# A transformer block's first attention block, paced by a fixed list of steps over 32 score pairs

## The chip, the core and the metric

The kernel runs on one core of one Trainium2 chip. Its time is device microseconds (us) for one launch. Three runs of the kernel before gave 1453.79, 1454.96 and 1455.0 us; their median, 1454.96 us, is what the change is compared with. Lower is better.

## The reference, cut to what matters

One transformer block on 2048 tokens of width 512: layer norm, attention with 32 query heads of 16 columns that share one key and one value head, a residual, layer norm again, a gated feed-forward part of width 1792, and a second residual.

```python
q = (x @ wq).reshape(B, S, H, Dh)          # x is the layer-normed input
k = x @ wk;  v = x @ wv                    # one K and one V head for all 32 query heads
scores = einsum("bhqd,bkd->bhqk", q, k) * (Dh ** -0.5)
o = einsum("bhqk,bkd->bhqd", softmax(scores), v)
h = x + o.reshape(B, S, H * Dh) @ wo
out = h + (gelu(ln(h) @ w_gate) * (ln(h) @ w_up)) @ w_down
```

All inputs and outputs are float32. The kernel splits most operands into a high and a low part, so that one projection takes three matmuls (high by high, high by low, low by high) for each 128 rows of depth.

## The kernel before, in words

The 2048 queries are cut into four blocks of 512 (`NB`, `T`). A prologue normalizes the input, makes K and V for all tokens and most of the queries of block 0. Then attention runs block by block. In a block there are 8 groups of four heads (`NG`), and in a group 16 chunks of 128 keys (`KC`). One chunk is two *score pairs*: `score(n)` (line 774) issues two matmuls into one score tile of PSUM (line 329) and one `exp` on ScalarE over 128x1024 scores (line 333). So a group is 32 score pairs and a block 256. There are three score tiles: two named `s` and, in the first block, a third (`s3`, line 324). ScalarE writes its result into an SBUF tile `p`, one for each chunk, of which there are five (`PB`).

A chunk whose two pairs are issued goes into the list `pend`. `finish(k)` (line 753) takes up to k chunks from its front and issues their *V-products* (`weigh`, line 335): four products of 512 columns, each of which the profile shows as two matmul instructions, so 8 for a chunk. All 16 chunks of a group add into one PSUM bank `acc`, of which there is one. After a group's last chunk `evacuate` (line 348) copies it on VectorE into `oT` (line 350), which leaves by DMA; a later DMA brings it back turned, and VectorE inverts the sums (line 366) and makes the split outputs `o_hi` and `o_lo`. Those steps wait in the list `outs` and are taken by `take_out`.

While block 0 attends, two more things are done beside it.

- The queries of blocks 1 to 3, and the rest of block 0, are projected by the generator `project_q` (line 170). Each 128 columns of `wq` (a piece `c`, four of them in a block) take 12 matmuls into one PSUM bank (`pq`; `width = 1`, so there is one such bank). The generator gives the word back after every three matmuls. After the last three, VectorE splits the bank into `qh` and `ql`, squares it into `qs`, and three DMAs on SyncE's queue store them. For the pieces in `HURRY` the bank is first copied to SBUF (`pq_raw`) and split from there. After a block's four pieces come the norm matmuls (`pqn`, line 218), which need all four `qs`, a copy `qn` and a maximum on VectorE, four small steps on GpSimd (`mm`, lines 227 to 234) and a last VectorE step `m` (line 245) that waits for them.
- `part_weights` (line 406) halves, splits and stores the feed-forward weights in 46 steps, all on GpSimd and its DMA queue. Their order in the program follows the score pairs (one step after every fourth pair but every 24th), but nothing in them waits for TensorE.

TensorE, ScalarE, VectorE, GpSimd and SyncE run in program order there, so the loop at line 811 sets what stands behind what. It works in fours of score pairs. Before the fourth pair of each four, if projection work is left, the generator is asked once: three matmuls, or a block's norm step. At the start it is asked twice before each of pairs 4, 6 and 8 (`RAMP`). After the fourth pair `finish` issues the V-products of all chunks but two, which is two chunks at a time. When no work is left, `finish(1)` also runs after the second pair of each four, so that the chunks go one by one.

The loop runs over block 0 and the first 16 pairs of block 1 (`lead`, 272 pairs). At pair 256 `drain` issues whatever projection work is left, the early tiles are closed, and four pairs later `dense(0)`, the output projection and feed-forward part of block 0, is set up. From pair 272 on a second loop (line 857) runs attention of blocks 1 to 3 with the dense work of the block before woven in, by fixed shares. The last dense block runs alone.

Of the kernel before, what the change touches and what calls it, by code (L numbers as in the profile page):

```python
# [29 lines left out]

HURRY = ((0, 3), (1, 0), (1, 1))

RAMP = {3: 2, 5: 2, 7: 2}

RUNS = ((0, 1, 2, 3), (4, 5, 6, 7), (8, 9, 10, 11), (12, 13))

# [6 lines left out]
def kernel(  # L43
# [23 lines left out]
    DC = D // P  # L67
    FC = F // P
    NG = H // 4
    KC = S // P  # L70
# [35 lines left out]
    def split(eng_hi, hi, lo, src, eng_lo=None):  # L106
        if eng_hi is nc.scalar:
            nc.scalar.activation(hi, src, AF.Copy)
        else:
            eng_hi.tensor_copy(hi, src)  # L110
        (eng_lo or nc.vector).tensor_tensor(lo, src, hi.bitcast(F32), op=ALU.subtract)  # L111
# [29 lines left out]
    def run(outer, first):  # L141
# [10 lines left out]
        def psum1(name):  # L152
            return ps.tile([P, T], F32, tag="d", bufs=width, name=name)
# [16 lines left out]
        def project_q(b, cs, eng, col):  # L170
            tsl = slice(b * T, (b + 1) * T)
            xT_hi, xT_lo = xT[b]
            urgent = b == 0 and cs[0] == 0
            qss = []
            for c in cs:
                pq = psum1(f"pq_{b}_{c}")
                n = 0
                for d in range(DC):
                    for wt, xt in ((wq_hi, xT_hi), (wq_hi, xT_lo), (wq_lo, xT_hi)):
                        nc.tensor.matmul(  # L180
                            pq, wt[:, d, c * P : (c + 1) * P], xt[:, d, :],
                            start=(n == 0), stop=(n == 3 * DC - 1),
                        )
                        n += 1
                    if urgent or d < DC - 1:
                        yield 3

                raw = None
                if (b, c) in HURRY:
                    raw = eb.tile([P, T], F32, tag="vT", bufs=3, name=f"pq_raw_{b}_{c}")  # L190
                    if b == 0:
                        nc.scalar.activation(raw, pq, AF.Copy)
                    else:
                        nc.vector.tensor_copy(raw, pq)
                    yield 3
                qh = eb.tile([P, T], F32R, tag="qh", bufs=2, name=f"qh_{b}_{c}")
                ql = eb.tile([P, T], F32R, tag="ql", bufs=2, name=f"ql_{b}_{c}")
                if raw is not None:
                    split(nc.vector, qh, ql, raw)
                else:  # L200

                    split(nc.vector if b == 0 and c == FIRST_Q else eng, qh, ql, pq)
                qs = eb.tile([P, T], BF16, tag="qs", bufs=DC, name=f"qs_{b}_{c}")
                (nc.gpsimd if urgent else nc.vector).tensor_tensor(
                    qs, qh.bitcast(F32), qh.bitcast(F32), op=ALU.mult
                )
                qss.append(qs)
                for r0, part in ((0, qh), (DH, ql), (2 * DH, qh)):
                    nc.sync.dma_start(
                        q_d[c * HC : (c + 1) * HC, r0 : r0 + DH, tsl].bitcast(F32),  # L210
                        part.bitcast(F32),
                    )
                if raw is None or b == 0:
                    yield 3

            pn = psum1(f"pqn_{b}_{cs[0]}")[:H, :]
            for i, c in enumerate(cs):
                nc.tensor.matmul(
                    pn, sel[:, c, :], qss[i], start=(i == 0), stop=(i == len(cs) - 1)
                )  # L220
            qn = eb.tile([H, T], F32, tag="qn", bufs=1, name=f"qn_{b}_{cs[0]}")
            nc.vector.tensor_copy(qn, pn)
            nc.vector.tensor_reduce(q2[:, col : col + 1], qn, axis=AX.X, op=ALU.max)
            yield 2

            mm = eb.tile([H, 3], F32, tag="mm", bufs=2, name=f"mm_{b}_{cs[0]}")
            nc.gpsimd.tensor_scalar(
                mm[:, 0:1], q2[:, col : col + 1], k2m, 1e-30, op0=ALU.mult, op1=ALU.add
            )
            nc.gpsimd.tensor_tensor(mm[:, 1:2], mm[:, 0:1], power[:H, 0:1], op=ALU.pow)  # L230
            nc.gpsimd.tensor_scalar(
                mm[:, 2:3], mm[:, 0:1], mm[:, 1:2], 0.5, op0=ALU.mult, op1=ALU.mult
            )
            nc.gpsimd.tensor_scalar(
                mm[:, 1:2], mm[:, 1:2], k2m, 0.5, op0=ALU.mult, op1=ALU.mult
            )
            m = eb.tile([H, T], F32R, tag="m", bufs=2, name=f"m_{b}_{cs[0]}")
            if urgent:
                nc.scalar.activation(
                    m, qn, AF.Identity, bias=mm[:, 2:3], scale=mm[:, 1:2]  # L240
                )
                ms[b] = m
                return
            yield 0
            nc.vector.tensor_scalar(m, qn, mm[:, 1:2], mm[:, 2:3], op0=ALU.mult, op1=ALU.add)
            hs = slice(cs[0] * HC, (cs[-1] + 1) * HC)
            nc.sync.dma_start(q_d[hs, 3 * DH, tsl].bitcast(F32), m[hs].bitcast(F32))
            yield 2
# [4 lines left out]

        def later_q():
            second = project_q(1, range(DC), nc.vector, 1)
            for _ in range(sum(RAMP.values())):
                yield next(second)

            next(q_rest)
            for _ in range(2 * DC - sum(RAMP.values())):  # L260
                yield next(second)
            yield from q_rest
            yield from second
            for b in range(2, NB):
                yield from project_q(b, range(DC), nc.vector, b)
            check_bound(eb, k2m)
# [68 lines left out]
        def weigh(acc, p, kc):  # L335
            for j in range(4):
                nc.tensor.matmul(  # L337
                    acc[32 * j : 32 * j + 32, :], v_sb[:, kc, :], p[:, j, :],
                    start=(kc == 0), stop=(kc == KC - 1), skip_group_check=True,
                )  # L340
# [63 lines left out]
        db = None  # L404
# [342 lines left out]
        PER = NG * KC  # L747
        work = None
        qgs = {(0, 0): qg_first if first else load_q(0, 0)}
        acc = None  # L750
        pend = []

        def finish(n):
            for _ in range(min(n, len(pend))):
                pb, pg, pkc, pp, pacc, _ = pend.pop(0)
                weigh(pacc, pp, pkc)
                if pkc == KC - 1:
                    evacuate(pb, pg, pacc)
# [44 lines left out]
        n, lead = 0, 2 * PER + sum(SIZES[: LEAD[0]])  # L803
        with tc.manual_schedule(engines={mybir.EngineType.SP, mybir.EngineType.DVE}):
            parts = None
            if first:
                work = later_q()
                parts = part_weights(early.enter_context(tc.tile_pool(name="parts", bufs=1)))


            while n < lead:
                if n == 2 * PER:
                    drain()
                    for _ in parts or ():
                        pass
                    parts = None
                    early.close()
                    db = late.enter_context(tc.tile_pool(name="dense", bufs=1))
                if n % 4 == 0:
                    given = work is not None  # L820
                for _ in range(RAMP.get(n, n > 7 and n % 4 == 3) if given else 0):
                    if next(work, None) is None:
                        work = None
                score(n)
                n += 1
                if n % 4 == 2 and not given and len(pend) > 2:
                    finish(1)
                if n % 4:
                    continue
                if len(pend) > 2:  # L830
                    finish(len(pend) - 2)
                if outs:
                    take_out()
                if parts is not None and n > 12 and n % 24:
                    next(parts, None)
                if n == 2 * PER + 4:
                    primed = dense(0)
                    next(primed)
        assert not outs
        work = primed  # L840
        set_banks("ps_rest")
# [15 lines left out]
        for c in range(LEAD[0], (NB - 1) * NG * len(SIZES)):  # L857
            b, cb = divmod(c, NG * len(SIZES))
# [4 lines left out]
            if b > 0 and cb == LEAD[b]:  # L863
                assert work is None
                work, todo = dense(b), list(kinds)
# [34 lines left out]
            if work is not None and not todo:  # L900
                assert next(work, None) is None
                work = None
# [259 lines left out]
    def check_bound(sb, k2m):  # L1162
        q2m = sb.tile([H, 1], F32, name="q2m")
        nc.vector.tensor_reduce(q2m, q2, axis=AX.X, op=ALU.max)
        nc.vector.tensor_tensor(q2m, q2m, k2m, op=ALU.mult)
        nc.sync.dma_start(b_d.rearrange("o h -> h o"), q2m)
# [77 lines left out]
```

## Time and profile before

The profiled execution took a span of 1453.0 us on the core; the median of the runs is 1454.96 us, so some 2 us lie outside the span or between executions.

| | before |
|---|---|
| median of 3 runs | 1454.96 us |
| span of the profiled execution | 1453.0 us |
| chain that ended last: TensorE / ScalarE / GpSimd / DMA | 65% / 16% / 6% / 5% |
| HBM read / written | 131.13 MB / 47.71 MB |
| mean granted TensorE clock | 0.998 |
| exp on ScalarE (line 333) | 1024 times, 969.0 us busy |
| V-products on TensorE (line 337) | 4096 instructions, 490.7 us busy |
| scores on TensorE (line 329) | 1984 instructions beside the 64 of the first group, 394.0 us busy |

How to read the views used below. The page's first part gives for each engine its busy time and the number of its instructions. A timeline row has the start and the length in us, the engine, the line of the kernel, the operation, the tiles written and read, their shapes, how many instructions were merged into the row, and in brackets how long the engine had been idle and whose result it then waited for. "PE" is TensorE's matmuls, "DVE" VectorE, "ACT" ScalarE, "POOL" GpSimd, "SPq" SyncE's DMA queue. Matmul lengths overlap with the next matmul, so that the time of a run of them is read from start to start. In a row of the score line, x2 is one score pair; in a row of the V-products, x8 is one chunk. A row of stretches gives start and end, the length, and then busy time and instructions of each engine.

### The profile page before, as it was taken

The numbers are of one execution on the slowest core, as the hardware profiler recorded it, in microseconds if no ns is written. First come the engines' busy times: TensorE is split into PE (matmuls) and PEld (weight loads), VectorE is DVE, ScalarE is ACT, GpSimd is POOL, SyncE is SP. The second block draws the span as 40 slices with busy tenths as digits, with TensorE's granted clock in tenths as the row PEclk, the third lists the DMA queues.
The fourth block names the chain that finished last, engine by engine and source line by source line (L and its number), as shares of the span: only waits on it lengthen the run. The fifth ranks groups of instructions, "written<-read, shape, count | busy, mean of one in ns | idle before, by whom it ended". The sixth has DMA issues, their size and how long they took to land.

```text
span 1453.0 us, 24765 instructions
## 1 busy us (share of the span) xinstructions
PE 1411.0 (97%) x10420; PEld 749.6 (52%) x10420; DVE 540.5 (37%) x925; ACT 1039.8 (72%) x1147; POOL 222.5 (15%) x305
## 2 busy tenths in 40 slices
PE   6999999999999999999999999999999999999998
PEld 5533333325555555554555555554455555556886
DVE  7422232313251424333241423323342422425665
ACT  6699999996777777776777777776777777772000
POOL 5477677721000000000000000000000000001000
PEclk9999999999999999999999999999999999999999
DMA  4465766642323332213332332203323222332552
GB/s 155 147 201 194 223 224 215 222 134 81 119 90 106 114 113 84 85 49 115 122 114 84 114 113 85 85 33 111 142 84 113 99 100 94 116 135 90 203 184 79
DMA packets 58863, 180.54 MB, mean 124 GB/s; under 512 B 8540, under 2 KB 8540, under 8 KB 51544
## 3 DMA queue, kind: packets, MB, share of 16 engines
q1 hardware_dynamic: 48912, 144.79, 29.6%
q0 software_dynamic: 9760, 34.08, 7.2%
q8 instruction: 84, 1.38, 0.4%
q14 instruction: 35, 0.29, 0.1%
q10 hardware_dynamic: 72, 0.00, 0.0%
HBM read 131.13 MB, written 47.71 MB: 123 GB/s over the span
## 4 chain that ended last, share of the span: by engine, by line
PE 65%; ACT 16%; POOL 6%; DMA 5%; issue 4%; DVE 2%; SPq 0%; ACTq 0%; POOLq 0%; DVEq 0%
PE acc L337 26%; ACT p L333 16%; PE s L329 14%; PE pu L490 5%; PE pd L490 5%; DMA w_1r<-in_B_w_up_dram 4%; PE pg L490 4%; PE pg L512 3%; PE pd L512 3%; PE pu L512 3%; PE pq L180 1%; PE pp L490 1%; POOL w_1b L111 1%; POOL w_d L433 1%; POOL w_0r L422 0%
## 5 line engine op out<-in xcount | busy, mean ns | idle before, releaser
L333 ACT ACTIVATE p<-s 128x1024 f32<-128x1024 f32 x1024 | 969.0, 1041 | 263.2 <-PE s L329 262.8
L337 PE MATMUL acc<-p,v_sb 128*32 128x512 f32 x4096 | 490.7, 598 | 0.2 <-DVE oT L350 0.2
L329 PE MATMUL s<-qg,kaug 50*128 50x512 f32 x1984 | 394.0, 436 | 18.5 <-ACT p L333 13.9
L329 PEld LDWEIGHTS s<-qg,kaug 50*128 50x128 f32 x1984 | 170.9, 184 | 307.6 <-ACT p L333 194.2
L337 PEld LDWEIGHTS acc<-p,v_sb 128*32 128x32 f32 x4096 | 110.7, 109 | 241.4 <-issue 232.3
L490 PE MATMUL pg<-x2h,w 64*128 64x512 f32 x672 | 231.7, 391 | 0.0
L490 PE MATMUL pu<-x2h,w 64*128 64x512 f32 x672 | 231.6, 391 | 0.0
L120 POOL TENSOR_SCALAR rstd<-mv 128x1 f32<-128x1 f32 x16 | 3.5, 218 | 1008.3 <-DVE mv L118 1008.1
L490 PE MATMUL pg<-x2l,w 64*128 64x512 f32 x336 | 131.3, 391 | 0.0
L490 PE MATMUL pu<-x2l,w 64*128 64x512 f32 x336 | 131.3, 391 | 0.0
L490 PEld LDWEIGHTS pu<-x2h,w 64*128 64x128 f32 x672 | 124.7, 186 | 11.3
L490 PEld LDWEIGHTS pg<-x2h,w 64*128 64x128 f32 x672 | 124.7, 186 | 10.8
L490 PE MATMUL pd<-w,gh 64*128 64x512 f32 x672 | 105.5, 391 | 0.0
L690 ACT ACTIVATE ga<-ga 128x512 f32<-128x512 f32 x56 | 36.2, 646 | 89.3 <-DVE ga L685 89.3
L682 DVE COPY g<-pg 128x512 f32<-128x512 f32 x56 | 38.5, 688 | 128.3 <-PE pg L490 121.2
L490 PEld LDWEIGHTS pd<-w,gh 64*128 64x128 f32 x672 | 63.3, 185 | 14.6 <-issue 0.7
L498 DVE COPY mark_pu<-pu 128x1 f32<-128x1 f32 x42 | 6.7, 158 | 166.9 <-PE pu L490 166.9
L691 DVE SCALAR_TENSOR_TENSOR ga<-ga,g 128x512 f32<-128x512 f32 x56 | 38.8, 692 | 79.7 <-ACT ga L690 79.7
L490 PE MATMUL pd<-w,gl 64*128 64x512 f32 x336 | 66.6, 393 | 0.0
L490 PEld LDWEIGHTS pg<-x2l,w 64*128 64x128 f32 x336 | 62.3, 185 | 7.3
L490 PEld LDWEIGHTS pu<-x2l,w 64*128 64x128 f32 x336 | 62.3, 185 | 7.2
L718 DVE TENSOR_TENSOR h<-h,pd 128x512 f32<-128x512 f32 x48 | 30.8, 684 | 90.2 <-PE pd L490 90.2
(235 smaller groups left out, 1313.4 us busy)
## 6 DMA issues: line engine op xcount, KB each, us to landing
w<-w_d SPq DMA_DIRECT2D x84, 1024.0 KB
qg<-q_d SPq DMA_DIRECT2D x62, 200.0 KB
q_d<-qh SPq DMA_DIRECT2D x32, 256.0 KB
acc_d<-oT SPq DMA_DIRECT2D x32, 256.0 KB
oc<-acc_d SPq DMA_DIRECT2D x128, 64.0 KB
w_d<-w_0b POOLq DMA_DIRECT2D x14, 512.0 KB, 5.6
w_d<-w_1b POOLq DMA_DIRECT2D x14, 512.0 KB, 3.8
x<-in_A_x_dram SPq DMA_DIRECT2D x16, 256.0 KB
```

Of the source, the lines that this page charges most:

```text
L111: (eng_lo or nc.vector).tensor_tensor(lo, src, hi.bitcast(F32), op=ALU.subtract)
L180: nc.tensor.matmul(pq, wt[:, d, c * P : (c + 1) * P], xt[:, d, :], start=(n == 0), stop=(n == 3 * DC - 1),)
L329: nc.tensor.matmul(s[:, a, :], kaug[rows, kc * P : (kc + 1) * P], qg[rows, u, :], start=True, stop=True,)
L333: nc.scalar.activation(p[:, 2 * u : 2 * u + 2, :], s, AF.Exp, scale=SCALE)
L337: nc.tensor.matmul(acc[32 * j : 32 * j + 32, :], v_sb[:, kc, :], p[:, j, :], start=(kc == 0), stop=(kc == KC - 1), skip_group_check=True,)
L433: nc.gpsimd.dma_start(w1_d[f, :, :, k].bitcast(F32), both.rearrange("p i (c n) -> p i c n", c=DC).bitcast(F32),)
L490: nc.tensor.matmul(banks[k], lhsT[rows], rhs[rows], start=(turn == 0 and i == 0), stop=(turn == 1 and i == n - 1), skip_group_check=True,)
L512: nc.tensor.matmul(bank, lhsT, rhs, start=(i == 0), stop=(i == len(ts) - 1))
L682: nc.vector.tensor_copy(g, pg)
L690: nc.scalar.activation(a, a, AF.Tanh, scale=GELU_A * GELU_C)
L691: nc.vector.scalar_tensor_tensor(a, a, 1.0, g, op0=ALU.add, op1=ALU.mult)
L718: nc.vector.tensor_tensor(hs[t], hs[t], pd, op=ALU.add)
```

## The change

The loop's rule by fours gives way to two strings. `OPENING` is run once and `PERIOD` eight times; a character is one step: `s` a score pair, `v` the V-products of one chunk, `p` a visit to the projections, `n` a block's norm step if one is due. `RAMP` goes, and the pairs after the strings' end up to `lead` keep to the old rule for when no projection work is left.

```diff
-RAMP = {3: 2, 5: 2, 7: 2}
+OPENING = "ssspsspsp"
+
+PERIOD = "ssvssvssvnssvvsssvsvssvssvvssspssvvsssvvsspsssvvsnssp"
...
                 if raw is None or b == 0:
-                    yield 3
+                    yield 4 if b > 0 and c == DC - 1 else 3
...
             second = project_q(1, range(DC), nc.vector, 1)
-            for _ in range(sum(RAMP.values())):
+            for _ in range(DC):
                 yield next(second)
 
             next(q_rest)
-            for _ in range(2 * DC - sum(RAMP.values())):
-                yield next(second)
             yield from q_rest
             yield from second
...
-            while n < lead:
+            normed = True
+
+            def visit():
+                nonlocal work, normed
+                total, k = 0, None
+                while work is not None and total < 6 and (k != 2 or last == 0):
+                    last, k = k, next(work, None)
+                    if k is None:
+                        work = None
+                        return
+                    total += k
+                normed = k != 4
+
+            def norm():
+                nonlocal normed
+                if not normed:
+                    next(work)
+                    normed = True
+
+            def pace():
+                nonlocal n, primed, parts, db
                 if n == 2 * PER:
                     drain()
...
-                if n % 4 == 0:
-                    given = work is not None
-                for _ in range(RAMP.get(n, n > 7 and n % 4 == 3) if given else 0):
-                    if next(work, None) is None:
-                        work = None
                 score(n)
                 n += 1
-                if n % 4 == 2 and not given and len(pend) > 2:
-                    finish(1)
                 if n % 4:
-                    continue
-                if len(pend) > 2:
-                    finish(len(pend) - 2)
+                    return
                 if outs:
                     take_out()
                 if parts is not None and n > 12 and n % 24:
...
+            primed = None
+            moves = {"s": pace, "p": visit, "n": norm, "v": partial(finish, 1)}
+            for step in OPENING + PERIOD * (PER // KC):
+                moves[step]()
+            while n < lead:
+                pace()
+                if n % 4 == 2 and len(pend) > 2:
+                    finish(1)
+                elif n % 4 == 0:
+                    finish(len(pend) - 2)
```

In `PERIOD` there are 32 `s`, 16 `v` in 11 runs (six of one chunk, five of two), 3 `p` and 2 `n`. A visit asks the generator until six matmuls are issued or a norm step ends it. `later_q` also moves the norm step of block 0's rest ahead: it comes after the first 12 matmuls of block 1, at pair 6. The value 4 that the last piece now gives back tells the visit that a norm step is due.

## The prediction, made before the changed kernel was run

> **What bounds the kernel now.** I read the page's first part, then the busy time by stretches, then the timeline of TensorE and ScalarE where the change works.
>
> ```profile
> span 1453.0 us, 24765 instructions
> PE 1411.0 (97%) x10420; PEld 749.6 (52%) x10420; DVE 540.5 (37%) x925; ACT 1039.8 (72%) x1147; POOL 222.5 (15%) x305
> ```
>
> TensorE is busy for 97% of the span, ScalarE for 72%. But the share is an average; the stretches (end, length, busy time by engine) differ:
>
> ```profile
> 72.00:140.00 68.00, 65.11 (x445) 24.11 (x445) 13.86 (x17) 63.29 (x68) 49.80 (x63) 1.00 0.62 201
> 250.00:300.00 50.00, 47.68 (x329) 16.20 (x327) 15.02 (x20) 47.56 (x52) 36.01 (x45) 1.00 0.70 216
> 350.00:400.00 50.00, 49.41 (x390) 25.59 (x388) 17.41 (x32) 38.38 (x42) 2.38 (x5) 1.00 0.31 109
> ```
>
> In the first two, which lie in block 0, TensorE and ScalarE are both nearly full (in 250 to 300, 47.7 and 47.6 of 50). In the third, behind it, TensorE alone is full, 49.4 of 50. So time saved in block 0 should stay saved: what follows is a line of TensorE work in unchanged order. The stretch that changes runs from the first score pair to the first product of the dense part:
>
> ```profile
> 52.50 1.03 PE L329 MATMUL s<-qg_first,kaug 50*128 50x512 f32 x6 [0.75 <-ACT pq_raw L192]
> ...
> 326.95 0.40 PE L490 MATMUL pp<-wo_hi,o_hi 64*128 64x512 f32 x2
> ```
>
> It lasts 326.95 - 52.50 = 274.45 us. What does it hold? In both programs, whose instruction orders I compared, 274 pairs, 134 chunks, 144 projection matmuls and 15 norm matmuls lie between these two rows; behind them TensorE's order is the same.
>
> A four of pairs with projection work:
>
> ```profile
> 100.73 1.92 PE L337 MATMUL acc<-p,v_sb 128*32 128x512 f32 x16
> 102.59 0.96 PE L329 MATMUL s<-qg,kaug 50*128 50x512 f32 x6
> 103.48 0.50 PE L180 MATMUL pq<-xT_hi,wq_hi 128*128 128x512 f32 x1
> 103.82 0.40 PE L180 MATMUL pq<-xT_lo,wq_hi 128*128 128x512 f32 x1
> 104.05 0.39 PE L180 MATMUL pq<-xT_hi,wq_lo 128*128 128x512 f32 x1
> 104.37 0.50 PE L329 MATMUL s<-qg,kaug 50*128 50x512 f32 x2
> 104.80 1.92 PE L337 MATMUL acc<-p,v_sb 128*32 128x512 f32 x16
> ```
>
> No row has a bracket, so TensorE never waits: 104.80 - 100.73 = 4.07 us for four pairs. Two without such work:
>
> ```profile
> 75.95 0.49 PE L329 MATMUL s<-qg_first,kaug 50*128 50x512 f32 x2 [0.71 <-ACT p L333]
> 76.37 1.92 PE L337 MATMUL acc<-p,v_sb 128*32 128x512 f32 x16
> 78.23 0.98 PE L329 MATMUL s<-qg_first,kaug 50*128 50x512 f32 x6
> 79.93 0.50 PE L329 MATMUL s<-qg_first,kaug 50*128 50x512 f32 x2 [0.73 <-ACT p L333]
> ...
> 78.85 3.77 ACT L333 ACTIVATE p<-s 128x1024 f32<-128x1024 f32 x4 [0.21 <-PE s L329]
> ```
>
> Here TensorE waits 0.7 us for ScalarE, and yet ScalarE idles 0.2 us: 3.98 us. And the end, when the projections are used up:
>
> ```profile
> 289.68 1.07 PE L337 MATMUL acc<-p,v_sb 128*32 128x512 f32 x8
> 290.67 0.74 PE L329 MATMUL s<-qg,kaug 50*128 50x512 f32 x4
> 291.34 1.07 PE L337 MATMUL acc<-p,v_sb 128*32 128x512 f32 x8
> ...
> 286.08 42.32 ACT L333 ACTIVATE p<-s 128x1024 f32<-128x1024 f32 x46 [0.18 <-PE s L329]
> ```
>
> 46 exps without a gap, 42.32 / 46 = 0.92 us each. That is ScalarE's own pace; TensorE needs 1.66 us for two pairs and a chunk (291.34 - 289.68), less than 1.84. So block 0 has long parts in which TensorE binds (1.02 us a pair), and parts in which ScalarE binds and TensorE waits. The change deals the same work out anew.
>
> **The change, part by part.** *Prices.* Start to start in the rows above: a pair behind another 0.23 us ((0.89 - 0.43) / 2), a projection matmul 0.23 (103.82 to 104.05). A first pair behind other work takes 0.43, so a change to scores costs 0.20; three projections take 0.89, so a change to them costs 0.20 too. Two chunks take 1.86, one 0.99: a chunk is 0.87, and the change to it 0.12. I use 0.86 and 0.13.
>
> *Fixed work:* 274 x 0.23 + 134 x 0.86 + 159 x 0.23 = 63.0 + 115.2 + 36.6 = 214.8 us, the norm matmuls at the projections' price:
>
> ```profile
> 71.17 0.82 PE L218 MATMUL pqn<-qs,sel 128*32 128x512 bf16 x3
> ```
>
> (three in 0.82 us, 3 x 0.23 and a change of 0.13.)
>
> *Changes of kind.* A run of V-products costs 0.13 in and 0.20 out, 0.33; a visit to projections or norms 0.40. Before there are 78 runs and 49 visits: 25.7 + 19.6 = 45.3. After, 93 runs and 28 visits: 30.7 + 11.2 = 41.9. This saves 3.4 us.
>
> *Waits before.* 274.45 - 214.8 - 45.3 leaves 14.3 us in which TensorE waited. Eight fours without projections (two behind each of the four norm steps) lose 3.98 - 2.98 = 1.0 each, where 2.98 is 1.86 + 0.43 + 3 x 0.23: 8.0. The 46 last pairs lose 42.3 - 23 x 1.66 = 4.1. 2.2 us stay unassigned.
>
> *Waits after.* In a period TensorE needs 32 x 0.23 + 16 x 0.86 + 18 x 0.23 + 11 x 0.33 + 3 x 0.40 = 30.1 us, ScalarE 32 x 0.92 = 29.4. They are balanced over a period, not inside it. In the 19 pairs from the third visit to the next period's first, TensorE has 10 chunks in 8 runs: 4.4 + 8.6 + 2.6 = 15.6 us against ScalarE's 17.5. In the other 13 pairs (6 chunks in 3 runs, 18 projections, 3 visits) it needs 14.5 against 12.0. So TensorE gets 1.9 us ahead and must be allowed to carry that lead over, or it waits. Three score tiles let it be two pairs, 1.84 us, ahead. Bounds: 0 to 1.9 us lost a period, 0 to 15 in all. I take 0.6, nearer zero since the tiles hold nearly the whole lead, but not zero since in the fours at 75.95 the tiles were full too and a run of two chunks still cost ScalarE 0.2. Eight periods: 4.8 us.
>
> *The norm step moved to pair 6.* It needs `qs` of a piece whose split is now issued only there, behind the copy of `pq_raw`:
>
> ```profile
> 57.54 0.69 DVE L194 COPY pq_raw<-pq 128x512 f32<-128x512 f32 x1 [5.72 <-PE pq L180]
> ...
> 59.34 0.69 DVE L204 TENSOR_TENSOR qs<-qh 128x512 bf16<-128x512 f32 x1
> ...
> 57.26 0.73 PE L329 MATMUL s<-qg_first,kaug 50*128 50x512 f32 x4
> ```
>
> The same four VectorE steps end at 60.03. TensorE reaches the norm matmuls after one pair, at about 57.26 + 0.43 = 57.7, and waits 2.3 us. Queued behind them are pairs 7 and 8 and the first chunk, and ScalarE, which by then has six exps (from 53.15, till about 58.7), runs dry. I count 2.3 in full; 0 if ScalarE's pace hides it.
>
> *GpSimd.* The weight steps need TensorE nowhere, so they don't get faster with it. If the norm chain stood behind them, VectorE would hold at `m`, and behind `m` the copy of `acc` and the split of the next `pq`. In the new order the chains stand later among the weight steps, the last behind all 46. But GpSimd itself lost time waiting for the earlier ones:
>
> ```profile
> POOL mm L227 <- DVE q L223: 5.4, 1, 5.4
> POOL mm L227 <- ACT p L333: 3.3, 1, 3.3
> ...
> 301.55 0.63 POOL L439 DMA_DIRECT2D w_d<-w213b  x1 [0.30 <-POOL w213b L111]
> ```
>
> At the old pace the weights end at 302.2. Pair 256, where the last chain is issued, comes at 52.5 + 266 x 256 / 274 = 301 by the sum below, so `m` is late by a microsecond or two at most, and by none if those 8.7 us fall away. Behind `m` stands the last copy of `acc`, whose way to the dense part was
>
> ```profile
> 314.43 0.69 DVE L350 COPY oT<-acc 128x512 f32<-128x512 f32 x1 [28.12 <-PE acc L337]
> 321.24 3.39 DVE L366 RECIPROCAL oc<-oc 128x128 f32<-128x128 f32 x4 [6.12 <-DMA oc<-acc_d]
> 325.85 0.69 DVE L111 TENSOR_TENSOR o_lo<-oc,o_hi 128x512 fp32r<-128x512 f32 x1
> ...
> 329.50 0.41 PE L490 MATMUL pp<-wo_hi,o_hi 64*128 64x512 f32 x2
> ```
>
> ready at 326.5, first used at 329.50 (the tenth product pair): 3.0 us of cover. I cost it at nothing; without the cover it is at most 3 us. SyncE's queue carries the same DMAs; those for `m` move behind other loads whose groups start 28 pairs, 26 us, later. Nothing.
>
> *Sum.* 214.8 + 41.9 + 4.8 + 2.3 + 2.2 (unassigned, kept) = 266.0 us against 274.45: 8.4 us less. The span of 1453.0 becomes 1444.6; the median of the runs is 1454.96, 1.96 more than that span, so the time forecast is 1446.6 us.
>
> **The rivals.** *A, only the changes of kind count.* TensorE waits as long as it did, 14.3 us, since runs and visits collide with the exps in the new list as in the old. Then 214.8 + 41.9 + 14.3 + 2.3 = 273.3, 1.1 us less: 1453.8 us. For it: tiles that were full and still let ScalarE idle. Against it: 12.1 of the 14.3 came from parts with no projection at all, and such a part is now at most 19 pairs long. [...]
>
> *B, the single projection bank, on the other side.* A piece now ends with one visit and the next begins with another; at seven such joints only six or seven pairs lie between them (at the others 19). The first matmul of the next piece waits till VectorE has taken `qh` and `ql` from the bank. Rows:
>
> ```profile
> 112.64 0.69 DVE L110 CAST qh<-pq 128x512 fp32r<-128x512 f32 x1 [14.23 <-PE pq L180]
> ...
> 113.97 1.60 DVE L204 TENSOR_TENSOR qs<-qh 128x512 bf16<-128x512 f32 x1
> ...
> PE pq L180 <- DVE pq_raw L194: 0.3, 1, 0.3
> ```
>
> From visit to visit six pairs take some 5.8 us (six of 266 / 274); the visit itself takes 6 x 0.23 + 0.40 = 1.8 of them, so 4.0 are left. Two steps of 0.69 fit. With a division in front (3.39 + 1.9 by the rows at 321.24 to 326.5) they don't: 5.3 + 1.4 = 6.7, or 2.7 us late. If that happened at all seven joints, 18.9 us are lost, and the result is 1446.6 + 18.9 = 1465.5. It turns the sign from 8.4 / 7 = 1.2 us a joint on. Against it: before, TensorE waited for this bank 0.3 us once, and only four divisions fall into the block. [...]
>
> *C, no wait left.* The tiles carry the whole lead and nothing unassigned remains: 214.8 + 41.9 + 2.3 = 259.0, 15.4 less: 1439.5 us. ScalarE's own floor, 274 x 0.92 = 252, lies below that.
>
> **How the numbers follow.** The forecast, 1441 to 1452, gets 0.72; A 0.10, B 0.08, C 0.10. About 0.2% (2.9 us) is what a measurement tells from no change, so A is "same", and the forecast and C are "faster": 0.82, 0.10, 0.08. The range 1440 to 1454 takes A in and leaves out B and the lower half of C, 0.13.
>
> **What would show it.** Right: the stretch from the first score to the first `pp` is 266 us; TensorE's wait for `exp` is spread in small pieces over the block; ScalarE's pace is even, near 0.96 us a pair, with no 46-exp run; a wait of about 2 us stands at the first `pqn`. Wrong: a wait of `pq` for VectorE (B), a long hold at `m` with TensorE idle after it, or a dense part that begins earlier and ends as before.

## The result, and the profile after

| | before | after |
|---|---|---|
| median of 5 runs, us | 1454.96 (1453.70 to 1456.55) | 1449.54 (1447.82 to 1450.27) |
| span of the profiled execution, us | 1453.0 | 1446.9 |
| first score to first `pp`, us | 274.45 | 266.40 |
| first `pp` to the end, us | 1126.05 | 1127.44 |

The ratio of the times is 0.9961, 95% interval 0.9948 to 0.9973: 5.4 us faster, 0.37%. The stretch that the change deals out anew came out as predicted, 266.40 us for 266.0, so 8.05 us shorter. The span gained only 6.1 of them. The rest of this section shows where the other 2 went.

The busy line of the page after, with its span, and the two stretches of block 0 (end, length, busy time of TensorE, its weight load, VectorE, ScalarE and GpSimd):

```profile
span 1446.9 us, 24766 instructions
PE 1406.3 (97%) x10420; PEld 749.3 (52%) x10420; DVE 533.4 (37%) x925; ACT 1038.8 (72%) x1147; POOL 223.1 (15%) x305
72.00:140.00 68.00, 67.89 (x465) 25.61 (x464) 15.93 (x22) 65.20 (x71) 55.32 (x66) 1.00 0.69 225
250.00:300.00 50.00, 49.95 (x352) 18.18 (x346) 9.86 (x14) 48.43 (x53) 25.73 (x29) 1.00 0.59 180
```

TensorE is now busy for 67.89 of 68 us (65.11 before) and 49.95 of 50 (47.68 before) and ScalarE too does more in the same time. TensorE's waits between 48 and 327 us (engine, line, whom it waited for: us in total, times, longest) are short:

```profile
PE s L329 <- ACT p L333: 2.0, 5, 0.7
PE pp L490 <- DVE o_hi L112: 1.1, 1, 1.1
PE pqn L220 <- DVE qs L206: 1.1, 1, 1.1
PE s L329 <- ACT pq_raw L194: 0.7, 1, 0.7
PE pqn L220 <- DVE pq_raw L196: 0.5, 1, 0.5
```

Before, the first of these was 7.2 us in 11 waits. Its five waits after all begin at 303.92 us or later, when no projection work is left. The third and fifth are the first norm step, now at pair 6. The second is new. ScalarE's timeline near the end, where 46 exps stood in one row before:

```profile
273.38 12.98 ACT L333 ACTIVATE p<-s 128x1024 f32<-128x1024 f32 x14 [0.32 <-PE s L329]
286.55 7.44 ACT L333 ACTIVATE p<-s 128x1024 f32<-128x1024 f32 x8 [0.19 <-PE s L329]
294.18 4.69 ACT L333 ACTIVATE p<-s 128x1024 f32<-128x1024 f32 x5 [0.19 <-PE s L329]
```

From 273.38 to 294.18 it does 22 exps in 20.8 us, 0.95 us each: the even pace that was expected, near its own 0.92. The projections now last nearly to the end of the block: the last norm step begins at 301.99 us instead of 270.32.

*Where the new wait comes from.* The timeline of SyncE's queue, then of VectorE, then of TensorE, all after (start, us, engine, line, operation, in brackets the idle time before it and who ended it):

```profile
306.78 0.34 SPq L249 DMA_DIRECT2D q_d<-m  x1
307.22 0.37 SPq L1188 DMA_DIRECT2D b_d<-q2m  x1
307.68 0.39 SPq L351 DMA_DIRECT2D acc_d<-oT  x1
314.58 1.25 SPq L361 DMA_DIRECT2D oc<-acc_d  x3
```

```profile
306.93 0.67 DVE L350 COPY oT<-acc 128x512 f32<-128x512 f32 x1
318.60 3.39 DVE L366 RECIPROCAL oc<-oc 128x128 f32<-128x128 f32 x4 [11.00 <-DMA oc<-acc_d]
322.75 0.43 DVE L112 CAST o_hi<-oc 128x512 fp32r<-128x512 f32 x1
```

```profile
319.46 0.40 PE L490 MATMUL pp<-wo_hi,o_hi 64*128 64x512 f32 x2
...
323.32 0.50 PE L490 MATMUL pp<-wo_hi,o_hi 64*128 64x512 f32 x2 [1.14 <-DVE o_hi L112]
```

`acc_d`, the last group's sums, goes out at 307.68, and `oc`, which reads it back, can be issued at 314.58 only: 6.9 us. Directly ahead of it stands `b_d`, the 32 numbers of the norm bound, 0.1 KB. Before the change `b_d` stood at the same place of an earlier group, where nothing waited for it:

```profile
285.69 0.33 SPq L1166 DMA_DIRECT2D b_d<-q2m  x1
286.34 0.34 SPq L351 DMA_DIRECT2D acc_d<-oT  x1
291.89 1.06 SPq L361 DMA_DIRECT2D oc<-acc_d  x2
...
315.15 0.35 SPq L351 DMA_DIRECT2D acc_d<-oT  x1
317.25 1.91 SPq L361 DMA_DIRECT2D oc<-acc_d  x4
```

5.55 us behind `b_d`, 2.10 for the last group without it. By themselves these rows don't show that `b_d` is the cause: the six earlier groups of before, with no `b_d` ahead of them, took 2.1 to 8.5 us from `acc_d` to `oc`, and the seven earlier ones after took 2.2 to 10.0, beside the stores of weights and queries. What sets the last group apart is that those have ended there, and only the small stores of `m` and `b_d` go ahead of `acc_d`; the experiments tell the two apart. With the late landing the last group's division starts 11.00 us after its copy instead of 6.12, and `o_hi` is 1.14 us late for the tenth pair of output projections.

*The sum.* 8.05 gained in the stretch; 0.56 lost ahead of it (first score at 53.06, before 52.50); 1.23 lost from the first `pp` to the last `acc_d` of the program (982.87 us from 319.46 to 1302.33, against 981.64 from 326.95 to 1308.59), of which 1.14 is the wait above; 0.16 lost in the last 144 us. That leaves 6.1. The 0.56 arises ahead of the list. TensorE has the same instructions there in the same order, but its early matmuls start 0.43 us apart at first and 0.23 us later on, and this step came later. The same place of the order before:

```profile
23.32 0.39 PE L1031 MATMUL pk<-xT_lo,wk_hi 128*128 128x512 f32 x1
23.55 0.39 PE L1031 MATMUL pk<-xT_hi,wk_lo 128*128 128x512 f32 x1
```

and after:

```profile
23.62 0.63 PE L1053 MATMUL pk<-xT_lo,wk_hi 128*128 128x512 f32 x1
24.04 0.63 PE L1053 MATMUL pk<-xT_hi,wk_lo 128*128 128x512 f32 x1
```

### The profile page after: what moved, and what is told of

Read it like the earlier page. It is cut to its first block, busy times and chain, and to the rows that moved or that the text cites. A ratio compares the mean times of both kernels' runs of the same rounds, so it can differ in the third digit from the quotient of the medians.

```text
span 1446.9 us, 24766 instructions
## 1 busy us (share of the span) xinstructions
PE 1406.3 (97%) x10420; PEld 749.3 (52%) x10420; DVE 533.4 (37%) x925; ACT 1038.8 (72%) x1147; POOL 223.1 (15%) x305
## 4 chain that ended last, share of the span: by engine, by line
PE 76%; ACT 16%; issue 3%; DVE 2%; DMA 1%; POOL 0%; SPq 0%; ACTq 0%; POOLq 0%; DVEq 0%
PE acc L337 31%; PE s L329 17%; ACT p L333 15%; PE pu L490 5%; PE pd L490 5%; PE pg L490 4%; PE pq L182 3%; PE pd L512 3%; PE pg L512 2%; PE pu L512 2%; PE pp L490 1%; PE pk L1053 1%; DMA acc_d<-oT 1%; DVE oc L366 0%; DMA w<-w_d 0%
## 5 line engine op out<-in xcount | busy, mean ns | idle before, releaser
L490 PEld LDWEIGHTS pg<-x2h,w 64*128 64x128 f32 x672 | 124.8, 186 | 10.6
L366 DVE RECIPROCAL oc<-oc 128x128 f32<-128x128 f32 x64 | 56.0, 919 | 37.4 <-DMA oc<-acc_d 36.3
```

The costliest lines, as they stand in the source:

```text
L366: nc.vector.reciprocal(oc[:, 1, sl], oc[:, 1, sl])
L490: nc.tensor.matmul(banks[k], lhsT[rows], rhs[rows], start=(turn == 0 and i == 0), stop=(turn == 1 and i == n - 1), skip_group_check=True,)
```

## The experiments

The theory: in block 0 TensorE and ScalarE need nearly the same time, three score tiles are all that one can be ahead of the other, so it counts where in the list V-products and projections stand, and not only how many runs of them there are. The rival is A of the prediction, by which only the count of changes decides. The last group's wait has a theory of its own: `b_d`. Where a run changes the list, a letter is a step: `s` a score pair, `v` a chunk, `p` a visit, `n` a norm step. The kernel before, run beside them, had medians of 1455.1 to 1456.3 us.

**V-products by twos again.** The visits of six stay spread over the block, but each four of pairs ends with a run of two chunks.

```diff
-PERIOD = "ssvssvssvnssvvsssvsvssvssvvssspssvvsssvvsspsssvvsnssp"
+PERIOD = "ssvvsssnsvvssspsvvssssvvssspsvvssssvvsssnsvvssspsvvss"
```

> Visits of six spread evenly as in the changed kernel, but the V-products by the old rule: two chunks behind every fourth pair. TensorE has 69 runs and 28 visits instead of 93 and 28, so 24 x 0.33 = 7.9 us less work. If only TensorE's work and its changes of kind count (rival A), the stretch from the first score to the first pp goes from 266.4 us to about 258.5. My theory, that the short runs of the list let ScalarE and TensorE overlap: five fours of a period without a visit take 3.98 us each as in the trace of before and three with a visit of six 4.75, 34.2 a period against 30.8 measured now, so up to 27 us more, less what is carried over: 276 to 293 us, slower than before.

1476.6 us, stretch 296.19, 3.2 above the upper end of the theory's range. A period holds 8 V runs instead of 11, so by the count it would be shorter; it is 30 us longer, and 21.7 longer than before the change, so with V-products by twos the spread visits are no gain. TensorE's timeline (matmuls of the visit left out) and ScalarE's:

```profile
107.25 0.50 PE L329 MATMUL s<-qg,kaug 50*128 50x512 f32 x2 [0.71 <-ACT p L333]
107.69 1.92 PE L337 MATMUL acc<-p,v_sb 128*32 128x512 f32 x16
109.54 0.97 PE L329 MATMUL s<-qg,kaug 50*128 50x512 f32 x6
...
112.02 0.50 PE L329 MATMUL s<-qg,kaug 50*128 50x512 f32 x2
```

```profile
110.14 3.77 ACT L333 ACTIVATE p<-s 128x1024 f32<-128x1024 f32 x4 [0.19 <-PE s L329]
114.91 3.77 ACT L333 ACTIVATE p<-s 128x1024 f32<-128x1024 f32 x4 [1.00 <-PE s L329]
118.87 3.77 ACT L333 ACTIVATE p<-s 128x1024 f32<-128x1024 f32 x4 [0.19 <-PE s L329]
```

A four with a visit takes 112.02 - 107.25 = 4.77 us: TensorE binds, and ScalarE idles 1.0. The next, without one, starts its exps at 114.91 and the one behind it at 118.87, 3.96 us apart: ScalarE binds, and TensorE waits 0.7 (a bracket like that at 107.25). Neither lends the other its idle time. Three fours of the one kind and five of the other are 34.1 us a period against 30.83 in the change. The other 5.5 us of the 30 is one place (its visits lie 18.2 us apart, others there 12.7), where a norm step's chain on GpSimd stood behind a weight step that itself waited 4.87 us for its data: VectorE held 4.94 us at `m`, and TensorE 3.46 us at the V-products behind it. So the loss by GpSimd that the prediction described, and costed at nothing, exists. In the change VectorE holds at `m` too, 7.24 us in the longest case, but no matmul of TensorE waits behind it.

**Visits of three.** The V runs stay; the visits are halved and doubled in number, 22 more in the block.

```diff
-PERIOD = "ssvssvssvnssvvsssvsvssvssvvssspssvvsssvvsspsssvvsnssp"
+PERIOD = "spsvssvssvnssvvsssvsvssvssvvssspssvvsspsvvsspsspsvvsnssp"
...
-                while work is not None and total < 6 and (k != 2 or last == 0):
+                while work is not None and total < size and (k != 2 or last == 0):
...
+            moves = {"s": pace, "p": partial(visit, 3), "P": partial(visit, 6), "n": norm, "v": partial(finish, 1)}
```

> The new list, but the projections in visits of three matmuls, twice as many and spread as evenly; V-products as in the changed kernel. 50 visits instead of 28, 22 x 0.40 = 8.8 us more TensorE work. My theory says that TensorE now binds on average over the block (30.1 us a period against ScalarE's 29.4), so the stretch grows by nearly all of it: 266.4 + 8.8 = 275 us, as long as before (274.5). If the gain came only from dealing the projections out over the whole block, it stays near 266.

1460.1 us (median of 10 runs; ratio 1.0032, interval 1.0019 to 1.0044): slower than before the change. The stretch is 280.85, 14.5 longer than with sixes and 6 more than I expected. 22 x 0.40 = 8.8 is what the visits should cost; 1.4 is a norm step that now follows its piece too soon:

```profile
128.34 0.81 PE L220 MATMUL pqn<-qs,sel 128*32 128x512 bf16 x3 [1.08 <-DVE ql L113]
129.45 0.38 PE L220 MATMUL pqn<-qs,sel 128*32 128x512 bf16 x1 [0.30 <-DVE qs L206]
```

Most of the rest is one place, which comes back in every period. Two pairs between a visit of three and a run of two chunks wait for `exp`:

```profile
112.67 0.50 PE L329 MATMUL s<-qg,kaug 50*128 50x512 f32 x2
113.46 0.50 PE L329 MATMUL s<-qg,kaug 50*128 50x512 f32 x2 [0.29 <-ACT p L333]
```

The chunks behind them start at 113.89, 1.22 us after 112.67, where two pairs take 0.66 elsewhere in this run (115.74 to 116.40): 0.56 lost, about 4.5 in eight periods. Less 1.4 and 4.5, and if all other waits stayed as they were, 8.6 us are left for the 22 visits, near the 8.8. So the count of changes matters too: where TensorE binds, each further visit costs some 0.4 us.

**Visits of twelve.** Eleven visits spared, each visit a whole piece.

```diff
-PERIOD = "ssvssvssvnssvvsssvsvssvssvvssspssvvsssvvsspsssvvsnssp"
+PERIOD = "ssvssvssvnssvvsssvsvssvssvvssspssvvsssvvsssssvvsnssp" \
+    "ssvssvssvnssvvsssvsvssvssvvsssssvvsssvvsspsssvvsnss"
...
-            moves = {"s": pace, "p": visit, "n": norm, "v": partial(finish, 1)}
-            for step in OPENING + PERIOD * (PER // KC):
+            moves = {"s": pace, "p": partial(visit, 12), "P": partial(visit, 6), "n": norm, "v": partial(finish, 1)}
+            for step in OPENING + PERIOD * (PER // KC // 2):
```

> Visits of twelve projection matmuls instead of six, eleven of them, with the V runs as in the changed kernel. Theory (TensorE and ScalarE in balance, the three score tiles as the only store): the eleven visits spared take 0.40 us each, 4.4 us, from TensorE, but a visit of about 3.2 us is longer than the 2.8 us for which two full score tiles feed ScalarE, so that each of the eleven stops ScalarE for some 0.5 to 1.5 us and the V runs behind come late: the stretch ends between 267 and 280 us, longer than 266.4. Rival (only the number of changes of kind counts, as in rival A of the prediction): 266.4 less 4.4, about 262 us.

1463.76 us, stretch 282.53: 16 longer, 2.5 beyond the theory's range, 20 from the rival's 262. ScalarE around the visit that starts at 117.50:

```profile
109.80 9.57 ACT L334 ACTIVATE p<-s 128x1024 f32<-128x1024 f32 x10 [0.19 <-PE s L330]
121.08 3.77 ACT L334 ACTIVATE p<-s 128x1024 f32<-128x1024 f32 x4 [1.71 <-PE s L330]
```

Twelve such waits, of 0.92 to 1.88 us, lie in the block behind the first norm step, 15.7 us together, and where there is no visit TensorE waits for `exp`, 13.2 us in 27 waits. Sixes lie between two losses: threes pay more changes, twelves outrun the tiles.

**Two score tiles.** The list of the change, without the third tile.

```diff
-            third = width == 1 and (2 * i + u) % 3 == 2
+            third = False
```

> The changed kernel without the third score tile. My forecast rested on three tiles that let TensorE run two pairs (1.84 us) ahead. With two it can be one pair ahead (0.92): in every period at least another 1.0 us of the 1.9 us lead is lost, and runs of two chunks and visits of six (1.9 and 1.8 us) each starve ScalarE by about one exp: 8 x 1.0 = 8 us more at least, up to 8 x 8 x 0.9 = 58 us (eight long steps a period). If the tiles don't carry the lead, the stretch stays at 266 us.

1511.38 us, stretch 329.08: 62.7 longer, 4.7 beyond the upper end. ScalarE's waits for scores go from 11.7 us in 37 to 69.2 in 95, TensorE's for `exp` from 2.0 in 5 to 46.0 in 68. The store between the two engines is what the list lives on.

**The bound stored later.** `q2m` gets a place of its own, and `b_d` is issued four pairs later, behind the last `acc_d`.

```diff
                 if n == 2 * PER + 4:
                     primed = dense(0)
                     next(primed)
+                    nc.sync.dma_start(b_d.rearrange("o h -> h o"), q2m)
...
-        nc.sync.dma_start(b_d.rearrange("o h -> h o"), q2m)
```

> The changed kernel, with the 128-byte DMA of the bound (b_d from q2m) issued four pairs later on SyncE's queue, behind the last group's way to and from DRAM in place of directly ahead of it. If that small store is what holds the landing of acc_d back (6.9 us instead of 2.1), oc is fetched 2.1 us behind acc_d, o_hi is ready some 4.8 us earlier, the 1.1 us wait of pp for o_hi goes, and the span is 1 to 1.5 us shorter with the stretch to the first pp unchanged. If the late norm step (the store of m) holds it, 6.9 us and the wait stay.

1446.74 us, span 1444.7, stretch 266.45. SyncE's queue:

```profile
307.67 0.35 SPq L351 DMA_DIRECT2D acc_d<-oT  x1
309.74 1.70 SPq L361 DMA_DIRECT2D oc<-acc_d  x4
...
314.14 0.43 SPq L850 DMA_DIRECT2D b_d<-q2m  x1
```

2.07 us instead of 6.9, and no wait for `o_hi`. The store of `m` still goes ahead of `acc_d`, so it isn't the cause. The span is 2.2 us shorter, more than the 1 to 1.5 expected. Of the 2.25 us by which the part behind the stretch is shorter, 0.92 lie between the first `pp` and the last `acc_d` of the program (981.95 us instead of 982.87); the other 1.33 are in the last 144 us, which vary by themselves (below).

**The bound on ScalarE's queue.** Is it SyncE's queue, or what lies behind it?

```diff
-        nc.sync.dma_start(b_d.rearrange("o h -> h o"), q2m)
+        nc.scalar.dma_start(b_d.rearrange("o h -> h o"), q2m)
```

> The changed kernel with the small store b_d issued from ScalarE's queue instead of SyncE's, at the same point of the program; it still starts ahead of the last acc_d, which stays on SyncE's queue. Theory 1 (the delay lies in the queue: a small store holds up what follows it on the same queue): acc_d lands after 2.1 us as in x4_bound_later, o_hi is in time, no wait at the output projections. [...]

ScalarE's and SyncE's queue:

```profile
306.43 0.36 ACTq L1188 DMA_DIRECT2D b_d<-q2m  x1
...
307.03 0.35 SPq L351 DMA_DIRECT2D acc_d<-oT  x1
313.12 1.71 SPq L361 DMA_DIRECT2D oc<-acc_d  x4
```

6.09 us, where 2.1 was expected if the delay lay in SyncE's queue: it comes with `b_d` on ScalarE's queue as well (6.9 us in the change). What carries it from the one queue to the other, no run shows, nor why 128 bytes do it. (No wait for `o_hi` shows, since ScalarE held 3.63 us at the issue and the stretch became 271.56; the time of 1451.01 says nothing else.)

**The first norm step later.** It moves from pair 6 to pair 8.

```diff
-            for step in OPENING + PERIOD * (PER // KC):
+            for step in OPENING[:-1] + PERIOD[:3] + "p" + PERIOD[3:] + PERIOD * (PER // KC - 1):
```

> The changed kernel with the first norm step three steps later (at the eighth pair instead of the sixth), nothing else. Theory: the 1.6 us for which TensorE stood at the first norm step, and the 1.96 us for which ScalarE then lacked scores, go; the stretch from the first score to the first output projection comes to about 265 us instead of 266.4, and the wait of 1.1 us for o_hi behind the stretch stays. Rival: VectorE, which casts the weights in these first 20 us, is late for the later place as well: the wait moves with the step and the stretch stays within 0.3 us of 266.4.

Stretch 264.58, span 1443.6, time 1445.73. TensorE and ScalarE after the change, at pair 6:

```profile
58.87 0.59 PE L220 MATMUL pqn<-qs,sel 128*32 128x512 bf16 x2 [0.52 <-DVE pq_raw L196]
60.53 0.38 PE L220 MATMUL pqn<-qs,sel 128*32 128x512 bf16 x1 [1.07 <-DVE qs L206]
...
61.37 7.44 ACT L333 ACTIVATE p<-s 128x1024 f32<-128x1024 f32 x8 [1.96 <-PE s L329]
```

and with the step at pair 8:

```profile
59.95 0.38 PE L220 MATMUL pqn<-qs,sel 128*32 128x512 bf16 x1 [0.18 <-DVE qs L206]
...
60.83 5.61 ACT L333 ACTIVATE p<-s 128x1024 f32<-128x1024 f32 x6 [0.16 <-PE s L329]
```

ScalarE's 1.96 becomes 0.16, and the stretch is 1.82 shorter: the wait was worth its whole length. VectorE does the same four steps, the first of them 5.06 and 5.09 us behind the first score; only what waits for them comes later. The wait for `o_hi`, which was to stay at 1.1 us, is 0.64.

**Both repairs.** The two edits above together.

> The changed kernel with both repairs: the small store b_d is issued four pairs after the bound is checked, and the first norm step stands three steps later in the opening (at the eighth pair). Theory: the two waits are separate terms and add: 1.1 us less in front of the first output projection (as in x4_bound_later, whose rest after the stretch was 1125.2 us) and 1.0 to 1.6 us less in the stretch (266.4 to about 265.1), so a span of 1443 to 1444 us and a time of 1445 to 1446 us. Rival: the wait at the first norm step only moves what ScalarE has to do anyway (VectorE is behind in the opening), the stretch stays at 266.4 and the span at 1444.7.

1445.97 us (median of 6 runs, 1444.95 to 1447.03); ratio to before 0.9933, interval 0.9917 to 0.9948. Stretch 264.73, no wait for `o_hi`, span 1442.9. That span, of the fastest of the six runs, is 0.1 below the expected 1443 to 1444, and the other five are 1443.5 to 1444.9; the time lies within its range. It is 9.2 us below before, where the change alone gave 5.4. That both edits together beat the first norm step's alone isn't shown: its single run took 1445.73.

**The change once more.**

> The changed kernel once more, unchanged, on the chip of these runs, as the measure for them. The stretch should repeat within 0.3 us of 266.4 and the wait for o_hi stand near 1.1 us; the first score is expected at 53.06 us if its later start belongs to this program, and anywhere from 52.4 to 53.1 if it varies from execution to execution.

1448.84 us, stretch 266.35, first score at 53.10, wait for `o_hi` 0.36 us with `acc_d` landing after 6.18. The stretch repeats to 0.05 us; the wait does not (1.14 us after, 0.64 with the norm step later, 0.36 here), since it hangs on how late `acc_d` lands (6.9, 6.4, 6.18). The first score stands at 53.10, where it would be if its later start belonged to this program; so that isn't ruled out (more below).

## Why the prediction was right, and where it was not

*The stretch.* 266.40 for 266.0, and the mechanism with it: waits in small pieces, ScalarE at 0.95 us a pair, no long run of exps at the end, a wait at the first norm step. The visits show the waits after: from visit to visit 7.52, 5.56 and 17.75 us, again and again, 30.83 a period against TensorE's 30.1, so 0.7 lost a period (0.6 taken), 5.8 in eight (4.8). They have no brackets of their own, but they can be read from start to start. Ahead of a period's third visit three pairs take 1.22 us, where 0.90 is usual (86.12 to 87.02):

```profile
88.87 1.29 PE L329 MATMUL s<-qg,kaug 50*128 50x512 f32 x6
90.09 0.50 PE L182 MATMUL pq<-xT_hi,wq_hi 128*128 128x512 f32 x1
```

Twice more, at 96.66 and 104.29, two pairs ahead of a run of two chunks take 0.80 instead of 0.66. Together that is 0.6 of the 0.7. The first norm step cost TensorE 1.6 us (2.3 taken), and its removal gained 1.8. With 214.8 + 41.9 of work, 9.7 us remain; 5.8 + 1.6 leave 2.3, where 2.2 was kept as unassigned. So the sum is right by its terms, with two errors of 1.0 and 0.7 that go against each other. The 2.2 itself agrees by luck. The trace of before has nine fours without projections that wait 0.7 us, not eight (the ninth waits at 283.20, ahead of the even pace at the end), so 1.2 was unassigned, and the sum with it would have been 265.0. Most of the 2.3 after are the five waits for `exp`, 2.0 us, in the last pairs, when no projection work is left; before, two such waits, 0.75 us, stood there.

*The prices* of changes agree with the run with threes, in which 8.6 us are left for 22 further visits at 0.40 each.

*The step that failed* is "I cost it at nothing", of the last group's way to the dense part, with "SyncE's queue carries the same DMAs … Nothing". The list of DMAs was the same, but not what stands ahead of the last `acc_d`: moving the last norm step put `b_d` there. `acc_d` still left 11.8 us ahead of the first `pp` (307.68 to 319.46; before 315.15 to 326.95). But it landed 4.8 us later (6.9 against 2.1). The late product waits for `o_hi`, which was ready 3.7 us ahead of its use before (325.85 to 329.50, the 3.0 of the prediction counting `o_lo` in): 4.8 - 3.7 = 1.1 us, the 1.14 on TensorE. The bound given without cover, 3 us, held. The trace of before had the warning: of its eight groups in block 0 five took 3.7 to 8.5 us to land, the one behind `b_d` 5.55, and the prediction passed over them since nothing waited for them there. The 2.1 of the last group was the case to explain.

*The rivals.* A fell: 266.4 is not 273.3, and with fewer V runs than the change the stretch became 30 us longer. B did not occur: no wait of `pq` for VectorE stands in the list after. C allowed no wait but the norm step's; the 5.8 of the periods and the 2.3 unassigned stand against it.

*The total.* 8.4 us were forecast and 5.4 measured (6.1 between the two profiled executions). The 2.3 missing between the profiles are the 1.23 behind the first `pp`, the 0.56 of the later first score, 0.16 at the end and the 0.4 by which the stretch is longer than the sum. 1449.54 lies within the forecast's own range of 1441 to 1452. The runs of the change spread over 2.5 us, and the profiled one, at 1448.96, was below their median.

## What to carry to other kernels

Where two engines are balanced over a period, as here with 30.1 us against 29.4, the order inside it can decide (the same matmuls and exps took 266.40 us in the change and 296.19 with V-products by twos): write down for each stretch between visits what each engine needs, and keep the difference below what the tiles between them can hold (one tile less made the stretch 62.7 us longer). When a step moves, look at what its DMAs land in front of: here, with a store of 128 bytes ahead of it, the last group's store of 256 KB landed after 6.9 us instead of 2.1, and after 6.09 with the small one on another queue, so keep such a store away from a transfer that somebody waits for. A price read where nothing waits is still a price: look for the slow instance in the trace before, and ask whether the change moves it to where it counts.

## What the runs showed of the hardware

*Behind a tiny store a large one landed later.* With `b_d`, 32 numbers of 4 bytes, issued 0.4 to 0.7 us ahead of it, the last group's 256 KB `acc_d` landed after 6.9, 6.18, 6.4, 5.85 and 5.62 us (after, the change once more, with the norm step later, with threes and with two tiles) and 6.09 (from the other queue); without them the same group's took 2.10 (before), 2.07 (bound later) and 2.07 (both repairs). It is not the only cause of a late landing: with V-products by twos this group took 6.62 with `b_d` 10.8 us ahead, and earlier groups, beside larger stores, up to 10.6. The time is not spent in moving data. The window of the change from 310 to 315 us, in which `acc_d` is awaited till 314.58 (the last two columns are the DMA engines' busy share and GB/s):

```profile
310.00:315.00 5.00, 5.00 (x40) 1.41 (x32) 0.00 (x0) 4.81 (x6) 0.00 (x0) 1.00 0.00 0
```

The busy share of the DMA engines is 0.00 and they move 0 GB/s, and yet `oc` can be issued at 314.58 only.

*TensorE's step to the quicker pace is not at a fixed time.* In eleven profiled executions the first quick matmul of 512 columns stands between 21.5 and 24.5 us, 3.0 us apart, though TensorE's work up to there is the same. The granted clock of the profile reads 1.00 on both sides of the step (in each stretch from 18 to 28 us, before and after), and the step shows in the matmuls' starts alone (0.43 and 0.23 us apart). Where it comes at 24.5 (four of them, both executions of the change among them) the first score is at 53.04 to 53.10 us, otherwise at 52.43 to 52.63. With two executions of the change, both late, and one of before, no run shows whether it hangs on the program, or what sets its time.

*The last 144 us vary by 3 us.* From the last `acc_d` to the end the profiled executions took 143.1 to 146.0 us in the same order of work. Two causes show in TensorE's rows, a weight that is late, here in the change, and eight matmuls at the slower pace, here before, where the granted clock from 1330 to 1335 us was 0.66:

```profile
1336.94 2.08 PE L512 MATMUL pg<-x2h,w 128*128 128x512 f32 x8 [1.53 <-DMA w<-w_d]
```

```profile
1330.74 3.44 PE L512 MATMUL pg<-x2h,w 128*128 128x512 f32 x8
```

The two nearly cancel between these executions, but a difference of 1 us between two single runs means nothing here; the stretch, which repeats to 0.05 us, is the better measure of an edit to block 0.
